# The last stage of a fused float32 kernel: two weight parts at a time, weights streamed in order of use, sums kept in PSUM, splits twice as wide

## The chip, the core and the metric

The kernel runs on one core of one Trainium2 chip. The metric is the device time of one execution in microseconds (us). TensorE multiplies (PE in the profile; its weight loads are PEld), VectorE (DVE), ScalarE (ACT) and GpSimd (POOL) work element by element, and SyncE (SP) issues the DMAs.

## What is computed

```python
x = attention(q, pooled k, pooled v)               # 8 batches x 576 tokens, 512 wide
x = ((x @ w1) * (x @ w2)) @ w3 @ w_out              # 4608 x 512
h = x @ w_in                                        # 512 -> 2048        the last stage
out = (h * sigmoid(1.702 * h)) @ w_out2             # 2048 -> 512
```

## The kernel before, in words

Only the last stage changes; everything before it issues the same instructions in both versions. Each float32 operand is kept as two parts, a rounded high part (a copy on ACT) and the rest (a subtraction on DVE): this pair of instructions is `split`, lines 104 and 105. A product is then three matmuls (high x high, high x low, low x high) of 128x128 weights with 512 moving columns: `mm3u`, line 706.

The stage takes nine blocks of 512 tokens. Block 0 is done plainly. The other eight are done as four **pairs** with a Strassen-Winograd scheme: each of the two layers needs seven products M1 to M7 in place of eight, with sums of the results between. A pair has two phases:

- The **first phase** (lines 922 to 973) loops over eight parts f of the hidden width. Per part each of M1 to M7 is 6 matmuls (two halves of 256 inputs, three matmuls each). Results are summed in four output blocks, go through gelu on ACT and become g11, g12, g22, g21; three differences of these are made on POOL (line 968). Between, M1 of the second layer runs, 12 matmuls for two parts (`m1_pair`).
- The **second phase** (lines 992 to 1039) runs the other six products of the second layer, 8 parts x 6 matmuls each. Its moving operands `mv` are splits of the g tiles, made by `make()` in a ring of NMV = 4 tiles, one part each.

Together a pair has 672 matmuls: 8 x 7 x 6 in the first phase and 7 x 8 x 6 in the second layer.

Weights come from DRAM in tiles `st` of 512 KB at most, in a ring of NST = 6 buffers: `stream()` lists them, and each `pull()` issues the next one on SP's queue, into the buffer used six tiles before. `win` tiles belong to the first layer, `wud` tiles to the second. While a pair's second phase runs, `x_prep` loads and splits the operands X of the next pair (tiles xM). Until the end of pair 1's first phase `w_sums` also prepares second-layer weights: load `u`, sums `ws`, and two results `wt` (cast on ACT, subtraction on DVE), each written to DRAM `wud` by DMA, from which later stages read it. A finished output is added and transposed on DVE into `ot` and stored.

A scheduler in the compiler's front end moves instructions on each engine's queue by its own estimate of times; a queue itself runs strictly in order.

## Time and profile before

| | us |
|---|---|
| median of three runs (lowest, highest) | 1592.86 (1592.41, 1598.03) |
| the profiled execution: its time, its span | 1596.34, 1594.6 |
| busy in the span: PE, PEld, DVE, ACT, POOL | 1476.6, 1200.8, 1033.9, 683.0, 672.0 |
| L706 waited until DVE's `mv` was done | 57.6 in 33 waits |
| L706 waited until DMAs of `st<-wud`, `st<-wind` landed | 48.3 in 25, 40.6 in 30 |

Matmuls overlap, so a busy PE may still run below its rate: a group of n matmuls is read by the distance from its start to the start of the next group. The granted clock (PEclk) is a share of 2.4 GHz; 0.5 is the lower level, 1.2 GHz.

### The profile page before, as it was taken

To read this page: it belongs to the slowest core of one execution; us is meant where nothing else is said; L and a number is where in the kernel's file an instruction comes from. 1 tells how busy PE (TensorE), PEld (TensorE's weight loads), DVE (VectorE), ACT (ScalarE), POOL (GpSimd) and SP (SyncE) were. 2 spreads that over 40 slices of the span, in tenths; PEclk is the share of its full clock that TensorE was granted. 3 is DMA by queue.
4 is the path that set the end of the run, shared out by engine and by line. 5 is a ranking of instruction groups with operands and counts; after the bars stand their busy time and mean duration, and the time that the engine had idled before them with its cause. 6 is when DMAs were issued, how large, how long until landed. Compare 5 with 4: busy or idle time off the path is not lost.

```text
span 1594.6 us, 19804 instructions
## 1 busy us (share of the span) xinstructions
PE 1476.6 (93%) x6536; PEld 1200.8 (75%) x6536; DVE 1033.9 (65%) x1868; ACT 683.0 (43%) x1304; POOL 672.0 (42%) x717
## 2 busy tenths in 40 slices
PE   5979999999999999999999888999879997999888
PEld 3757888888888888888887766777658775777766
DVE  7888997888778774556453568733495246843465
ACT  6974444333434343655442234422343234423333
POOL 8788765555554453659131234013230233103340
PEclk9999999999999999999999998999999998999999
DMA  9991323222323102998897776665557555665455
GB/s 279 231 205 33 88 57 59 66 68 56 71 46 78 39 35 76 326 341 288 287 392 213 248 251 190 204 198 172 187 173 205 176 168 184 185 201 165 159 178 139
DMA packets 290023, 267.67 MB, mean 168 GB/s; under 512 B 199296, under 2 KB 223872, under 8 KB 289920
## 3 DMA queue, kind: packets, MB, share of 16 engines
q1 hardware_dynamic: 289344, 265.35, 55.9%
q8 instruction: 52, 0.85, 0.2%
q10 hardware_dynamic: 576, 1.05, 0.2%
q14 instruction: 51, 0.42, 0.1%
HBM read 209.72 MB, written 56.62 MB: 167 GB/s over the span
## 4 chain that ended last, share of the span: by engine, by line
PE 71%; DMA 11%; DVE 11%; issue 2%; ACT 2%; POOL 1%; SPq 0%; DVEq 0%; ACTq 0%; POOLq 0%
PE bk L706 32%; PE wk L114 7%; PE wk L116 7%; PE wk L115 7%; DMA st<-wind 4%; PE acc L114 4%; PE acc L116 4%; PE acc L115 4%; DMA st<-wud 3%; DVE mv L105 2%; PE wk L278 2%; DVE xM L105 1%; DMA wud<-wt 1%; DMA m<-x2d 1%; POOL cv L172 1%
## 5 line engine op out<-in xcount | busy, mean ns | idle before, releaser
L706 PE MATMUL bk<-mv,st 128*128 128x512 f32 x1152 | 301.8, 419 | 47.7 <-DMA st<-wud 23.6
L706 PEld LDWEIGHTS bk<-mv,st 128*128 128x128 f32 x1152 | 231.4, 204 | 111.3 <-DMA st<-wud 24.7
L706 PE MATMUL bk<-xM,st 128*128 128x512 f32 x1056 | 255.6, 393 | 24.7 <-DMA st<-wind 20.0
L706 PEld LDWEIGHTS bk<-xM,st 128*128 128x128 f32 x1056 | 197.6, 189 | 75.2 <-DMA st<-wind 20.5
L114 PE MATMUL wk<-s,s 128*128 128x512 f32 x576 | 228.0, 397 | 6.4 <-DVE a L641 3.8
L116 PE MATMUL wk<-s,s 128*128 128x512 f32 x576 | 225.0, 391 | 1.0 <-DVE s L105 1.0
L115 PE MATMUL wk<-s,s 128*128 128x512 f32 x576 | 225.3, 392 | 0.1
L105 DVE TENSOR_TENSOR mv<-g,mv 128x512 fp32r<-128x512 f32 x192 | 151.3, 796 | 103.8 <-ACT mv L104 103.7
L314 DVE STREAM_TRANSPOSE p<-s_t 32x160 f32<-32x160 f32 (+1 forms) x560 | 178.5, 319 | 10.5
L968 POOL TENSOR_TENSOR g<-s,g 128x512 f32<-128x512 f32 x32 | 43.7, 1365 | 331.0 <-ACT s L849 329.7
L104 ACT CAST mv<-g 128x512 fp32r<-128x512 f32 x192 | 118.6, 620 | 106.9 <-PE bk L706 66.3
L116 PE MATMUL acc<-s,s 128*128 128x512 f32 x352 | 139.8, 397 | 2.0 <-DVE s L105 2.0
L115 PE MATMUL acc<-s,s 128*128 128x512 f32 x352 | 139.9, 397 | 1.3 <-POOL s L105 1.1
L114 PE MATMUL acc<-s,s 128*128 128x512 f32 x352 | 131.9, 400 | 8.1 <-DVE s L105 5.3
L105 POOL TENSOR_TENSOR s<-a,s 128x512 fp32r<-128x512 f32 x56 | 73.4, 1310 | 155.2 <-ACT s L104 121.4
L114 PEld LDWEIGHTS wk<-s,s 128*128 128x128 f32 x576 | 108.7, 189 | 30.8 <-DVE a L641 5.0
L116 PEld LDWEIGHTS wk<-s,s 128*128 128x128 f32 x576 | 108.4, 188 | 23.8 <-DVE s L105 1.2
L115 PEld LDWEIGHTS wk<-s,s 128*128 128x128 f32 x576 | 108.6, 189 | 22.2 <-DVE s L391 0.5
L172 POOL TENSOR_TENSOR cv<-cv,s 128x512 int32<-128x512 int32 x72 | 100.8, 1408 | 34.5 <-DVE cv L169 23.8
L968 POOL TENSOR_TENSOR g<-g,g 128x512 f32<-128x512 f32 x32 | 44.8, 1401 | 148.1 <-ACT g L849 147.1
L114 PEld LDWEIGHTS acc<-s,s 128*128 128x128 f32 x352 | 66.9, 191 | 22.9 <-ACT s L104 4.9
L116 PEld LDWEIGHTS acc<-s,s 128*128 128x128 f32 x352 | 67.1, 191 | 15.6 <-DVE s L105 2.9
(197 smaller groups left out, 2497.1 us busy)
## 6 DMA issues: line engine op xcount, KB each, us to landing
st<-wud SPq DMA_DIRECT2D x96, 512.0 KB, 4.0
st<-wind SPq DMA_DIRECT2D x85, 512.0 KB, 4.5
s<-in_moe_w_dram SPq DMA_DIRECT2D x32, 512.0 KB, 6.7
wind<-s SPq DMA_DIRECT2D x32, 512.0 KB, 5.4
s<-wind SPq DMA_DIRECT2D x27, 512.0 KB, 4.9
s<-in_moe_w_out_dram SPq DMA_DIRECT2D x24, 512.0 KB, 6.8
kr<-in_k_dram SPq DMA_DIRECT2D x128, 72.0 KB, 2.5
qr<-in_q_dram SPq DMA_DIRECT2D x128, 72.0 KB, 2.5
```

Source lines behind the costliest of these rows:

```text
L104: nc.scalar.copy(dst[:, 0], src)
L105: lo_eng.tensor_tensor(out=dst[:, 1], in0=src, in1=f32(dst[:, 0]), op=ALU.subtract)
L114: nc.tensor.matmul(o, a[:, 0, a_sl], b[:, 0, b_sl], start=first, stop=False)
L115: nc.tensor.matmul(o, a[:, 0, a_sl], b[:, 1, b_sl], start=False, stop=False)
L116: nc.tensor.matmul(o, a[:, 1, a_sl], b[:, 0, b_sl], start=False, stop=last)
L172: nc.gpsimd.tensor_tensor(out=w.bitcast(I32), in0=w.bitcast(I32), in1=lo_w.bitcast(I32), op=ALU.add)
L278: nc.tensor.matmul(sc[half][:, i * KW:(i + 1) * KW], qT[:, sl(tt)], mov, start=True, stop=True)
L314: nc.vector.transpose(out=dst[:, :nt, 32 * c:32 * c + 32], in_=s_t[32 * c:32 * c + 32, :nt, 32 * r:32 * r + 32])
L706: nc.tensor.matmul(o, w[:, x, m], b[:, y], start=first and n == 0, stop=last and n == 2, skip_group_check=True)
L968: nc.gpsimd.tensor_tensor(out=o, in0=p, in1=m, op=ALU.subtract)
```

## The change

The first phase takes two parts at once: index i is 0 or 1, and the order is the new `ORDER`, in which "O" is M1 of the second layer. M6, M7 and M4 add onto the PSUM bank of M1, and M3 onto that of M5; ACT copies the sum out after M1 (`m`), M6 (`u`) and M7 (`m`). DVE makes three sums per part where it made five. `mv`, and the tiles of g and X, hold two parts, so that casts, subtractions, gelu (but for g21) and POOL's differences work on 1024 columns; g21 has its difference with t2 in four instructions (`t4`) and not eight. Weight tiles are listed in the order of use; those of M7, M4 and M3 are filled by two DMAs of half the size, one per part. The second phase begins with M2 in place of M6. `x_prep` gives one step per group of 12 matmuls unless a step of an output (`late`) is due. `ot`, shared with `wt`, has one buffer in place of two; `ws` and the raw weights `wq` use tiles of g.

```diff
+                    n = 0
                     for src in srcs:
-                        nc.sync.dma_start(f32(t[:, :src.shape[1]]), src)
+                        nc.sync.dma_start(f32(t[:, n:n + src.shape[1]]), src)
+                        n += src.shape[1]
...
-            return pb.tile([P, 2, T], F32R, name="mv", tag=f"mv{i}")
+            return pb.tile([P, 2, 2, T], F32R, name="mv", tag=f"mv{i}")
...
-            return pb.tile([P, T // 32, 2, 32], F32, name="ot", tag="ot", bufs=2)
+            return pb.tile([P, T // 32, 2, 32], F32, name="ot", tag="ot")
...
-        ORDER = (("M1", A11, 0, True), ("M6", S2, 1, True), ("M5", S1, 2, True), ("M7", S3, 1, False),
-                 ("M2", A12, 0, False), ("M4", A22, 1, False), ("M3", S4, 2, False))
-        HS = {A11: (0, 0), A12: (0, 1), S1: (1, 0), S2: (1, 1), S3: (2, 0), S4: (2, 1), A22: (3, 0)}
-        OUT = (("M6", S2), ("M2", A12), ("M7", S3), ("M5", S1), ("M4", A22), ("M3", S4))
+        ORDER = (("M1", 0), ("M1", 1), ("M2", 0), ("M2", 1), ("M6", 0), ("M5", 0), ("M6", 1),
+                 ("M7", 0), ("M5", 1), ("M7", 1), ("M4", 0), ("O", 0), ("M4", 1), ("M3", 0),
+                 ("M3", 1))
+        PART = {"M1": ("a", 0), "M2": ("a", 1), "M5": ("s", 0), "M6": ("s", 1)}
+        OUT = (("M2", A12), ("M6", S2), ("M5", S1), ("M7", S3), ("M4", A22), ("M3", S4))
...
+            for fp in range(NFP):
+                fs = (2 * fp, 2 * fp + 1)
+                for f in fs:
+                    stream(("a", pr, f), win_d[f][:, A11:A12 + 1])
+                for f in fs:
+                    stream(("s", pr, f), win_d[f][:, S1:S2 + 1])
+                stream(("M7", pr, fp), *(win_d[f][:, S3:S3 + 1] for f in fs))
+                stream(("M4", pr, fp), *(win_d[f][:, A22:A22 + 1] for f in fs))
+                if fp < NFP - 1:
+                    stream(("o", pr, "M1", fp), wu_d[A11][:, 2 * fp:2 * fp + 2])
+                stream(("M3", pr, fp), *(win_d[f][:, S4:S4 + 1] for f in fs))
             for n, (name, u) in enumerate(OUT):
-                for f in range(0, NP1, 2):
-                    stream(("o", pr, name, f // 2), wu_d[u][:, f:f + 2])
-                    if n == 0 and f == 0:
-                        stream(("o", pr, "M1", NP1 // 2 - 1), wu_d[A11][:, NP1 - 2:])
+                for fp in range(NFP):
+                    stream(("o", pr, name, fp), wu_d[u][:, 2 * fp:2 * fp + 2])
+                    if n == 0 and fp == 0:
+                        stream(("o", pr, "M1", NFP - 1), wu_d[A11][:, NP1 - 2:])
...
+            def load():
+                for name in ("M1", "M7", "M2", "M3", "M5", "M6", "M4"):
+                    X[name] = pb.tile([P, 2, 2, T], F32R, name=f"x{name}", tag=f"x{name}")
+                for name, c, b in (("M1", 0, b0), ("M7", 0, b0 + 1), ("M3", 2, b0 + 1),
+                                   ("M2", 2, b0)):
+                    nc.sync.dma_start(lo(name), x2_d[b][:, c:c + 2])
...
+            def diff(j, name, p_, m_):
+                if j not in sums:
+                    sums[j] = pb.tile([P, T], F32, name="sx", tag="sx")
+                s = sums[j]
                 nc.vector.tensor_tensor(
...
+                    out=s, in0=lo(p_, j), in1=lo(m_, j) if m_ else s, op=ALU.subtract)
+                split(X[name][:, :, j], s, nc.vector)
+
+            steps = [load]
+            for j in range(2):
+                for args in (("M5", "M7", "M1"), ("M6", "M3", None), ("M4", "M2", None),
+                             ("M7", "M3", "M7")):
+                    steps.append(lambda j=j, args=args: diff(j, *args))
+            return steps + [lambda name=name: resplit(X[name], nc.vector)
+                            for name in ("M1", "M2", "M3")]
...
+                raw["w"] = pb.tile([P, 2, T], F32, name="wq", tag="g15")
...
-                c = raw["c"] = pb.tile([P, 4, HU], F32, name="ws", tag="ot", bufs=2)
+                c = raw["c"] = pb.tile([P, 4, HU], F32, name="ws", tag="g11")
...
-                t = pb.tile([P, 2, 2, HU], F32R, name="wt", tag="ot", bufs=2)
+                t = pb.tile([P, 2, 2, HU], F32R, name="wt", tag="ot")
...
-            if k >= 6 and k % 2 == 0 and len(wsum) > 4 * (NP1 - 2):
...
+                g11, g12, g22, g21, t2 = (gtile(a * NFP + fp) for a in range(5))
+                G.append((g11, g12, g22, g21, t2))
+                C, Z, W = [None] * 2, [None] * 2, [None] * 2
+                m1, U, V = [None] * 2, [None] * 2, [None] * 2
...
+                for name, i in ORDER:
+                    if name == "O":
+                        if fp < NFP - 1:
+                            if fp == 0:
+                                bA += [bank() for _ in range(2)]
+                            out_mm(bA, "M1", fp, fp == 0, False)
+                        continue
...
+                    bs = W if name == "M2" else Z if name in ("M5", "M3") else C
+                    first = name in ("M1", "M2", "M5")
+                    if first:
+                        bs[i] = bank()
...
                     if name == "M1":
-                        m1 = tmp("m1", 2)
-                        nc.scalar.copy(m1, o)
+                        m1[i] = tmp("m")
+                        nc.scalar.copy(m1[i], o)
+                    elif name == "M2":
+                        ready.pop(("a", pr, 2 * fp + i))
+                        pull()
+                        nc.vector.tensor_tensor(out=g11[:, i], in0=o, in1=m1[i], op=ALU.add)
+                        freed(W[i])
+                        if i:
+                            gelu(g11, g11)
+                            g = mvs["M1", fp] = moving()
+                            split(g, g11, nc.vector)
                     elif name == "M6":
-                        tt = tmp("tt", 1)
-                        nc.vector.tensor_tensor(out=tt, in0=o, in1=m1, op=ALU.add)
+                        U[i] = tmp("u")
+                        nc.scalar.copy(U[i], o)
                     elif name == "M5":
-                        if f and f % 2 == 0:
-                            m1_pair(f // 2 - 1)
+                        ready.pop(("s", pr, 2 * fp + i))
+                        pull()
                     elif name == "M7":
-                        q_ = tmp("q", 1)
-                        nc.vector.tensor_tensor(out=q_, in0=o, in1=m1, op=ALU.add)
-                        nc.vector.tensor_tensor(out=g22, in0=B[2][1], in1=q_, op=ALU.add)
-                        gelu(g22, g22)
+                        V[i] = tmp("m")
+                        nc.scalar.copy(V[i], o)
+                        nc.vector.tensor_tensor(out=g22[:, i], in0=Z[i][1], in1=V[i], op=ALU.add)
+                        if i:
+                            gelu(g22, g22)
+                    elif name == "M4":
+                        gelu(g21[:, i], o)
+                        freed(C[i])
+                    elif name == "M3":
+                        nc.vector.tensor_tensor(out=g12[:, i], in0=o, in1=U[i], op=ALU.add)
+                        freed(Z[i])
+                        if i:
+                            gelu(g12, g12)
+                    if i and name in ("M7", "M4", "M3"):
+                        ready.pop((name, pr, fp))
                         pull()
...
+                    if wsum and (name, i) in (("M2", 1), ("M5", 0), ("M7", 0), ("M4", 0),
+                                              ("M6", 1), ("M7", 1), ("M4", 1)):
+                        wsum.pop(0)()
...
+            src = {"M5": 0, "M7": 1, "M3": 2, "M2": 3, "M4": 3, "M6": 4}
+            todo_mv = [(name, fp) for name, _ in OUT for fp in range(NFP)]
+            t4 = list(range(NFP))
 
             def make():
                 if todo_mv:
...
+                    name, fp = todo_mv.pop(0)
+                    g = mvs[name, fp] = moving()
+                    split(g, G[fp][src[name]], nc.vector)
+                    if t4 and (name, fp) in (("M6", 0), ("M6", 2), ("M5", 0), ("M5", 2)):
+                        t = G[t4.pop(0)]
+                        nc.gpsimd.tensor_tensor(out=t[3], in0=t[3], in1=t[4], op=ALU.subtract)
...
+                bs = bW if name == "M2" else bZ if name in ("M5", "M3") else bA
+                for fp in range(NFP):
+                    out_mm(bs, name, fp, name in ("M2", "M5") and fp == 0, fp == NFP - 1)
+                    make()
+                    if name == "M2" and fp == 0:
+                        out_mm(bA, "M1", NFP - 1, False, True)
                         for m in range(2):
-                            m1.append(tmp("ma", 2))
+                            m1.append(tmp("m"))
                             nc.scalar.copy(m1[m], bA[m][1])
-                        for _ in range(NMV):
-                            make()
-                    elif name != "M6" or f:
                         make()
+                    if late:
+                        late.pop(0)()
+                    elif prep:
+                        prep.pop(0)()
```

**SP's queue in the first phase of pair 2**, before: tiles are `st` or `s4` with a number, wind2 and wind3 are parts f = 2 and 3, 128x1024 is a whole tile and 128x512 half of one.

```order
L700 DMA st_9695<-wind2_76 128x1024
L700 DMA st_9683<-wud0_98 128x1024
L700 DMA st_9641<-wind2_76 128x1024
L700 DMA s4_9631<-wind2_76 128x1024
L700 DMA st_9784<-wind3_77 128x512
L700 DMA st_9772<-wind3_77 128x1024
L700 DMA st_9715<-wind3_77 128x1024
L700 DMA st_9705<-wind2_76 128x512
L700 DMA s4_9760<-wind3_77 128x1024
L700 DMA st_9846<-wud0_98 128x1024
```

The same place now:

```order
L702 DMA st_9472<-wind2_76 128x1024
L702 DMA st_9498<-wind3_77 128x1024
L702 DMA st_9510<-wind2_76 128x1024
L702 DMA s4_9542<-wind2_76 128x512
L702 DMA s4_9542<-wind3_77 128x512
L702 DMA st_9533<-wind3_77 128x1024
L702 DMA st_9560<-wind2_76 128x512
L702 DMA st_9560<-wind3_77 128x512
L702 DMA st_9596<-wud0_98 128x1024
L702 DMA st_9606<-wind2_76 128x512
L702 DMA st_9606<-wind3_77 128x512
```

Before, the tile of M7 and M3 of part 2 (`st_9695`) is issued ahead of that of its M1 and M2 (`s4_9631`), and those of part 3's M4 and M7 (`st_9784`, `st_9772`) ahead of its M1's (`st_9715`). Now both tiles of M1 and M2, then those of M5 and M6, M7, M4, wud0 and M3 follow each other nearly as they are used.

**DVE's queue where pair 2 passes to its second phase**, before, from the last sum of the first phase on (m1, q, tt, xM belong to the next pair's `x_prep`):

```order
L963 TENSOR_TENSOR g7_10138<-bk1_10137,tt_10154 128x512
L105 TENSOR_TENSOR xM30_10421<-q_10276,xM30_10421 128x512
L105 TENSOR_TENSOR mv_10295<-g8_9575,mv_10295 128x512
L778 TENSOR_TENSOR m1_10270<-m1_10272,m1_10270 128x512
L105 TENSOR_TENSOR mv_10307<-g9_9650,mv_10307 128x512
L778 TENSOR_TENSOR m1_10272<-q_10276,m1_10272 128x512
L105 TENSOR_TENSOR xM50_10351<-m1_10270,xM50_10351 128x512
L105 TENSOR_TENSOR mv_10346<-g12_9887,mv_10346 128x512
L778 TENSOR_TENSOR q_10276<-q_10276,m1_10270 128x512
L105 TENSOR_TENSOR xM20_10495<-tt_10274,xM20_10495 128x512
L105 TENSOR_TENSOR xM70_10389<-m1_10272,xM70_10389 128x512
L105 TENSOR_TENSOR mv_10286<-g19_10051,mv_10286 128x512
```

Now, from the same sum on (sx and xM are `x_prep`, `m` and `ot` the output of M2; mv_10058 is the fourth tile of M2, mv_10108, mv_10128 and mv_10150 the second, third and fourth of M6):

```order
L976 TENSOR_TENSOR g7_9877<-bk3_9958,u_9947 128x512
L105 TENSOR_TENSOR mv_10058<-g15_9879,mv_10058 128x1024
L105 TENSOR_TENSOR mv_10108<-g17_9570,mv_10108 128x1024
L792 TENSOR_TENSOR sx_10090<-xM3_10064,sx_10090 128x512
L105 TENSOR_TENSOR mv_10128<-g18_9725,mv_10128 128x1024
L105 TENSOR_TENSOR xM6_10066<-sx_10090,xM6_10066 128x512
L1017 TENSOR_TENSOR m_10054<-bk0_10021,m_10054 128x512
L792 TENSOR_TENSOR sx_10090<-xM2_10063,sx_10090 128x512
L730 STREAM_TRANSPOSE ot_10135<-m_10054 128x16x32
L1017 TENSOR_TENSOR m_10056<-bk1_10022,m_10056 128x512
L105 TENSOR_TENSOR mv_10150<-g19_9880,mv_10150 128x1024
```

Four splits of 512 columns stood among seven instructions of `x_prep`; now four of 1024 stand among three of `x_prep` and three of an output, and the first tiles of M2 and of M6 are made further ahead.

**TensorE's queue at the same place now**, behind the last M3 (its first row): the rest of M1, then M2 (bk0, bk1) with the first tile of M6 (bk6, bk7) between; five matmuls of that tile follow, and then M6's second tile, mv_10108.

```order
L709 MATMUL bk3_9958<-xM3_8937,s4_9906 128x512 x6
L709 MATMUL bk7_9520<-mv_9921,st_9939 128x512 x2
L709 MATMUL bk0_10021<-mv_10018,st_9965 128x512 x6
L709 MATMUL bk1_10022<-mv_10018,st_9965 128x512 x6
L709 MATMUL bk0_10021<-mv_10037,st_9977 128x512 x6
L709 MATMUL bk1_10022<-mv_10037,st_9977 128x512 x6
L709 MATMUL bk0_10021<-mv_10058,st_9993 128x512
L709 MATMUL bk1_10022<-mv_10058,st_9993 128x512
L709 MATMUL bk6_9519<-mv_10086,s4_10010 128x512 x6
L709 MATMUL bk7_9520<-mv_10086,s4_10010 128x512
L709 MATMUL bk0_10021<-mv_10058,st_9993 128x512 x5
L709 MATMUL bk1_10022<-mv_10058,st_9993 128x512 x5
```

Before, M6 stood first, on a source that POOL's last difference gives; now M2 does, on g21.

**ACT's queue in pair 1's first phase now**; a `wt` cast needs the one buffer that the one before filled and DMA emptied:

```order
L831 CAST wt_8354<-ws_8323 128x2x256
L968 COPY m_8472<-bk6_8385 128x512
L968 COPY m_8495<-bk7_8394 128x512
L858 ACTIVATE g9_8382<-g9_8382 128x1024
L831 CAST wt_8428<-ws_8323 128x2x256
L950 COPY m_8578<-bk4_8571 128x512
L858 ACTIVATE g13_8383<-bk6_8385 128x512
L858 ACTIVATE g13_8383<-bk7_8394 128x512
L104 CAST mv_8891<-g13_8383 128x1024
L831 CAST wt_8475<-ws_8461 128x2x256
```

Ten such casts stand among the copies and gelus of the second to the fourth two parts; before, twelve stood in the phase, with two buffers that they shared with `ws` and `ot`.

## Rows read from the trace of the kernel before

**Rows 1.** Timeline of PE: start, length, group of matmuls, count, idle before it.

```profile
857.38 7.87 PE L706 MATMUL bk<-xM,st 128*128 128x512 f32 x34
1201.40 13.76 PE L706 MATMUL bk<-mv,st 128*128 128x512 f32 x60
1215.00 2.88 PE L706 MATMUL bk<-mv,s 128*128 128x512 f32 x12
1579.28 8.32 PE L706 MATMUL bk<-mv,st 128*128 128x512 f32 x36
```

**Rows 2.** Engines by stretch: length, busy (count) of PE, PEld, DVE, ACT, POOL; PEclk, DMA.

```profile
1049.00:1136.00 87.00, 77.74 (x336) 62.16 (x334) 33.09 (x47) 27.48 (x46) 25.65 (x19) 1.00 0.59 184
1150.00:1185.00 35.00, 25.24 (x91) 18.28 (x90) 32.42 (x38) 16.77 (x30) 17.18 (x11) 0.90 0.55 175
1185.00:1219.00 34.00, 34.00 (x150) 27.82 (x149) 24.34 (x39) 15.53 (x25) 0.00 (x0) 1.00 0.75 217
1519.00:1546.00 27.00, 22.71 (x83) 16.85 (x83) 18.21 (x18) 9.37 (x16) 16.91 (x11) 0.87 0.45 149
```

**Rows 3.** Timeline of PE, pairs 1 and 2: single waits.

```profile
934.62 1.61 PE L706 MATMUL bk<-xM,st 128*128 128x512 f32 x6 [1.69 <-DVE tt L941]
...
1088.59 9.80 PE L706 MATMUL bk<-xM,st 128*128 128x512 f32 x42 [1.00 <-DMA st<-wind]
...
1136.83 4.59 PE L706 MATMUL bk<-mv,st 128*128 128x512 f32 x12 [3.07 <-DMA st<-wud]
...
1165.41 4.04 PE L706 MATMUL bk<-mv,st 128*128 128x512 f32 x10 [3.34 <-DVE mv L105]
```

**Rows 4.** Timeline of SP's queue: the issue before that wait for wud.

```profile
1132.42 0.32 SPq L700 DMA_DIRECT2D st<-wud  x1
```

**Rows 5.** DMA issues: out<-in, count, KB each, median us to landing.

```profile
st<-wud SPq DMA_DIRECT2D x96, 512.0 KB, 4.0
st<-wind SPq DMA_DIRECT2D x85, 512.0 KB, 4.5
...
wud<-wt SPq DMA_DIRECT2D x32, 256.0 KB, 4.4
st<-wind SPq DMA_DIRECT2D x32, 256.0 KB, 3.5
```

**Rows 6.** Timeline of DVE in pair 2, then of POOL there.

```profile
1156.12 1.77 DVE L105 TENSOR_TENSOR mv<-g,mv 128x512 fp32r<-128x512 f32 x1
...
1186.59 1.88 DVE L105 TENSOR_TENSOR mv<-g,mv 128x512 fp32r<-128x512 f32 x3
...
1155.61 1.74 POOL L968 TENSOR_TENSOR g<-g,g 128x512 f32<-128x512 f32 x1
1157.30 1.75 POOL L968 TENSOR_TENSOR g<-g 128x512 f32<-128x512 f32 x1
```

**Rows 7.** Single lines: duration ns lowest/median/highest, first and last start.

```profile
L968 POOL TENSOR_TENSOR g<-g,g x32: 1261/1287/1737, 934.0 to 1523.9; 128x512 f32<-128x512 f32 x32
L1023 DVE TENSOR_TENSOR u<-bk,ma x8: 675/677/678, 987.6 to 1532.8; 128x512 f32<-128x512 f32 x8
L104 ACT CAST mv<-g x192: 602/622/627, 865.7 to 1582.2; 128x512 fp32r<-128x512 f32 x192
L938 ACT COPY m<-bk x32: 581/589/590, 858.7 to 1492.6; 128x512 f32<-128x512 f32 x32
```

**Rows 8.** Timeline of ACT in pair 1's first phase: the `wt` casts, first and last four.

```profile
864.35 0.62 ACT L822 CAST wt<-ws 128x512 fp32r<-128x512 f32 x1 [0.97 <-DMA out_dram<-ot]
...
925.25 0.62 ACT L822 CAST wt<-ws 128x512 fp32r<-128x512 f32 x1 [2.91 <-DMA wud<-wt]
931.29 0.62 ACT L822 CAST wt<-ws 128x512 fp32r<-128x512 f32 x1 [3.90 <-DMA wud<-wt]
937.14 0.62 ACT L822 CAST wt<-ws 128x512 fp32r<-128x512 f32 x1 [2.20 <-DMA wud<-wt]
943.05 0.62 ACT L822 CAST wt<-ws 128x512 fp32r<-128x512 f32 x1 [1.17 <-DMA wud<-wt]
```

More of the change, by code (lines that the diff above doesn't have):

```diff
@@ L906, in pooled_attention_moe_moe2, with out_mm @@
             X = xc.pop(pr)
[L907 to L908 removed]
+            bA = []
+            G = []
             mvs = {}
[L911 to L912 removed]
+            def out_mm(bs, name, fp, first, last):
+                g, w = mvs.pop((name, fp)), ready.pop(("o", pr, name, fp))
                 for m in range(2):
[L914 to L920 removed]
@@ L922, in pooled_attention_moe_moe2 @@
-            for f in range(NP1):
-                B = [bank() for _ in range(3)]
-                ga.append(gtile(f))
-                gb.append(gtile(NP1 + f))
-                if f % 2 == 0:
-                    gc.append(gtile(2 * NP1 + f // 2))
-                g12, g22, g11, g21 = ga[f][:, 0], ga[f][:, 1], gb[f][:, 0], gb[f][:, 1]
-                t2 = gc[f // 2][:, f % 2]
-                for name, u, b, first in ORDER:
-                    o = B[b][1]
-                    s, h = HS[u]
-                    w = ready["h", pr, f, s]
+                    for i in range(2):
+                        mm3u(bs[m][1], w[:, i], m, g[:, :, i], first and i == 0, last and i == 1)
@@ L971, in pooled_attention_moe_moe2 @@
[L971 to L973 removed]
+            while wsum:
+                wsum.pop(0)()
             prep = x_prep(pr + 1) if pr < NPAIR else []
[L977 to L980 removed]
+            src = {"M5": 0, "M7": 1, "M3": 2, "M2": 3, "M4": 3, "M6": 4}
@@ new lines, in pooled_attention_moe_moe2, with out_of, part, end @@
+            late = []
+            def out_of(name, bs):
+                ot = out_tile()
+                add, blk, i = {"M2": (m1, b0, 0), "M7": (V, b1, 1),
+                               "M4": (None, b0, 1), "M3": (U, b1, 0)}[name]
+                def part(m):
+                    if add:
+                        nc.vector.tensor_tensor(out=add[m], in0=bs[m][1], in1=add[m], op=ALU.add)
+                    turn_out(ot, m, add[m] if add else bs[m][1])
+                def end():
+                    part(1)
+                    store(ot, blk, i)
+                return [lambda: part(0), end]
@@ L1040, in pooled_attention_moe_moe2 @@
+                        nc.scalar.copy(V[m], bA[m][1])
+                if name in ("M2", "M7", "M4", "M3"):
+                    late += out_of(name, bZ if name == "M7" else bs)
+                if name == "M2":
+                    freed(*bW)
+                elif name == "M4":
+                    freed(*bA)
+            while late:
+                late.pop(0)()
+            freed(*bZ)
             while prep:
```

140 lines of the change are left out of this document (27 added, 113 removed).

## The prediction

> **What bounds the kernel now.** I read the timeline of TensorE first. The last stage's four pairs begin at 857.38 and their last matmul group begins at 1579.28 and ends at 1587.60, so they take 730.2 us [rows 1]. Where nothing waits, 60 matmuls take 1215.00 - 1201.40 = 13.60 us, 0.2267 us each, at full clock [rows 1]. Four pairs of 672, less the one that had run before 857.38, are 2687 matmuls: 609.1 us. TensorE is the bound, and 121.1 us of these stages, 30 a pair, are not its work. An earlier stage cannot change, as its queues are the same.
>
> The table by stretch shows where pair 2 loses its share [rows 2]. Its first phase ran 336 matmuls (76.2 us) in 87.0: 10.8 lost. The start of the second phase ran 91 (20.6 us) in 35.0: 14.4 lost. After that 150 matmuls took 34.0, which is the price: nothing lost. The rest of the 30, some 5 us, goes where the phases meet. Pair 4 has no next pair to prepare; its start lost 27.0 - 83 x 0.2267 = 8.2.
>
> Then the single waits [rows 3]. In the first phase TensorE waits about 1 us at a time for `st<-wind`, and 3.07 us for `st<-wud` at 1136.83. SP issued that tile only at 1132.42 [rows 4]; a tile lands in 4.0 to 4.5 us [rows 5], so it was late because its buffer came free late, not because the transfer was slow. At the second phase's start TensorE waits for `mv` from DVE, 3.34 us once, and behind that wait 10 matmuls took 4.04 us where the price is 2.3 [rows 3]: the stretch from 1150 to 1185 has a granted clock of 0.90 [rows 2], so after such waits part of the work ran at the lower level of 1.2 GHz. A wait removed gives more than its own length.
>
> **What the change does to each.**
>
> *Weights in the first phase.* The six buffers now go round in order of use. The tightest tile is the first of M1: its buffer comes free when M5 has used it, and from there to its use lie some 25 matmuls, 5.7 us, against 4.5 us to land [rows 5]. The others have 36 matmuls (8.2 us) or more. The half-size DMAs are priced by the 256 KB row, 3.5 us [rows 5]; two issued one behind the other stay under 8.2. So the waits for `st` go to nothing. Bound on the other side: they stay as they are, 10.8 us a pair.
>
> *Sums in PSUM.* Three hand-offs per part now go from TensorE to ACT and back: the copies of M1, M6 and M7 must be out before the bank is added to. A copy takes 0.59 us [rows 7]; at least two other products, 12 matmuls or 2.7 us, stand between in the new order. Cost nothing; what hides it is that order, and ACT being free. ACT's first-phase work for two parts is 8 instructions of 0.59 to 0.62 us and four double ones of at most 1.24 [rows 7], at most 10 us in 21.8 (96 matmuls). DVE has six sums of 0.68 us [rows 7] and two double splits, below 7 us.
>
> *The second phase's start.* M2 goes first, on g21, which is long there, so the wait for POOL's last difference goes. What is late next is M6. I take the end of the last M3 as time 0 and go down the queues. TensorE: the new order puts 50 matmuls before M6's second tile (due at 11.3), 12 more before the third (14.1), and 77 before the low part of the fourth (17.5). DVE: a split of 512 columns takes 0.60 (three in 1.88 [rows 6]), a double one at most 1.2. POOL: 1.29 a difference [rows 7], doubled at most 2.6, I take 2.4; four of them run from 3.4 on. And DVE and POOL wait for each other: a split that meets a POOL difference took 1.77, POOL's own took 1.74, in turns [rows 6], while DVE sums that read PSUM never took over 0.68 [rows 7]. So each SBUF instruction of DVE waits for the POOL one that runs. In turns this gives: M2's fourth tile done at 3.4, M6's second at 7.0, `sx` at 9.9, M6's third at 13.4 (due 14.1), then one subtraction behind the fourth difference at 16.3, four instructions of the output and `sx` without POOL to 18.7, M6's fourth at 19.9: 2.4 late. From there DVE needs 2.4 us per group of 2.72 and catches up. Taken: 2.5 us in each of pairs 1 to 3, 0 in pair 4, which has no `x_prep`. Ends: 0, and the 14.4 of today.
>
> The Trainium skill states the same in "SBUF — State Buffer", section "SBUF: two separate sides": GpSimd and a VectorE instruction with two SBUF inputs take a shared pair of ports as an exclusive lock for the whole instruction, and the other blocks fully. The rows agree (1.77 against 0.60). By that rule wide differences speak against this change, as each holds the lock twice as long: were all four to block a split that is due, a start would lose 4 x 2.4 = 9.6 in place of 2.5, and the forecast below would be 21 us higher, 1519.
>
> *One buffer for `wt`.* In pair 1 a cast must wait until DMA has emptied the buffer: cast 0.62 [rows 8], subtraction as long as a sum, 0.68 [rows 7], two issues of 0.32 [rows 4], landing 4.4 [rows 5], 6.4 us with the hand-offs. Today, with two buffers shared, the last casts came every 5.9 us and the twelve of the phase took 864.35 to 943.05, on average 7.2 [rows 8]. Now ten of them stand in ACT's queue from the second two parts on, about 24 us into the phase (96 matmuls and the gelus behind them): the tenth falls at 24 + 9 x 6.4 = 81.6, while TensorE, unhindered, wants the copies behind it after 315 matmuls, at 71. ACT is in order, so M1, M6 and M7 of the last two parts queue behind it: 11 us lost, in pair 1 alone. Ends: 0 (6 us cycles, slack at the copies) and 22.
>
> *The rest.* One buffer for `ot` is emptied between two outputs 10.9 us apart; nothing. X is ready early, since `x_prep` now ends some 10 groups before the pair does. The tail after the last matmul keeps its two sums, two transposes and a store. Small waits at phase changes remain: my estimate is 2 us a pair of the 5 that go there today, 8 in all.
>
> **The sum.** 121.1 goes; 11 + 3 x 2.5 + 8 = 26.5 stays or is new: 94.6 less than the profiled execution's 1596.3, which is 1501.7. The median stands 3.5 below that execution, so I forecast **1498 us**.
>
> **Rivals.**
>
> 1. *Everything hidden.* The `wt` casts find slack and the locks fall between: 10 us remain of 121, giving 1593 - 111 = 1482. For it: after 1185 the second phase loses nothing today [rows 2]. Against: ten serial round trips.
> 2. *DVE and POOL keep the start of the second phase as it is.* Turns at twice the width cost as much as today, 3 x 14.4 + 8.2 = 51, with `wt` and small waits 70: 1593 - 51 = 1542. For it: DVE is busy 32.4 of 35.0 us there [rows 2]. Against: today that stretch has far more of `x_prep`. This is the case that the lock rule of that page supports.
> 3. *Slower: the hand-offs to ACT.* Six copies per two parts, 96 in the four pairs, and TensorE may not go on with a bank until ACT has copied it. The nearest row for such a hand-off that fails is 1.69 us, where M7 had to wait for a DVE sum that M6's bank needed [rows 3]. If ACT's queue, held by a cast or gelu of twice the width, left each hand-off uncovered by that much, 96 x 1.69 = 162 us would come and 121 go: 1634. It decides from 121 / 96 = 1.26 us per hand-off. Against it: 2.7 us of other matmuls before each.
> 4. *The first phase keeps its weight waits*, since DMAs land slower in halves: 43 us of the gain gone, 1541; with half of rival 2 1560.
>
> **How the numbers follow.** The forecast (1487 to 1520) has 0.50, everything hidden (below 1487) 0.14, rivals 2 and 4 (1520 to 1560) 0.26, no change 0.04, slower by the hand-offs 0.06. The measurement can tell about 0.5%, 8 us. So faster 0.90, same 0.04, slower 0.06. The range of 8 in 10 leaves out the slow cases (0.10), the top of rivals 2 and 4, and a little below: 1478 to 1545. The likeliest case's own range is 1487 to 1520; its ends are the bounds of `wt` (0 to 22) and some 10 us of locks.
>
> **What would show it.** Right: no wait for `st` of over 0.5 us in the first phases of pairs 2 to 4; pairs 2 and 3 take 156 to 160 us each; pair 1 is the longest by about 10, its waits ending on ACT's copies behind a `wt` cast that waits for `wud<-wt`; PEclk 1.00 in most of the stretch. Wrong: DVE splits of over 3 us beside POOL and a TensorE wait for `mv` in the second phase of over 5 us (rival 2); TensorE waiting for ACT `m` or `u` in every part (rival 3); waits for `st<-wind` (rival 4).

## The result and the profile after

The changed kernel takes **1496.72 us** (median of 4 runs, 1491.15 to 1500.06) against 1593.47 us for the kernel before: a ratio of 0.9384, with a 95% interval of 0.935 to 0.9418. The profiled execution took 1496.2 us, its span 1494.0.

The timeline of PE, rows that answer to [rows 1]: the first matmul group of each pair, then the last group.

```profile
856.46 5.38 PE L709 MATMUL bk<-xM,st 128*128 128x512 f32 x23
...
1023.85 1.52 PE L709 MATMUL bk<-xM,s 128*128 128x512 f32 x6
...
1179.86 11.04 PE L709 MATMUL bk<-xM,st 128*128 128x512 f32 x48
...
1335.36 5.60 PE L709 MATMUL bk<-xM,st 128*128 128x512 f32 x24
...
1474.08 13.76 PE L709 MATMUL bk<-mv,st 128*128 128x512 f32 x60
```

The four pairs take 631.4 us in place of 730.2. At 152.3 us of matmuls a pair (672 at 0.2267 us) the loss, which is the time of a pair above its matmuls, is now 15.1 us in pair 1, 3.7 in pair 2, 3.2 in pair 3 and 0.2 in pair 4: 22 in place of 121.

The table by stretch, as in [rows 2]: pair 2's first phase up to its only wait, the start of its second phase, and pair 4's start.

```profile
1024.00:1099.00 75.00, 75.00 (x333) 62.12 (x332) 25.21 (x29) 30.82 (x42) 26.26 (x11) 1.00 0.65 196
...
1115.00:1150.00 35.00, 33.49 (x147) 27.19 (x146) 32.02 (x31) 19.51 (x25) 11.90 (x4) 1.00 0.73 235
...
1425.00:1452.00 27.00, 27.00 (x121) 22.37 (x120) 19.68 (x15) 13.06 (x14) 11.46 (x4) 1.00 0.77 242
```

333 matmuls in 75.0 us of the first phase are the price and no more; before, 336 took 87.0. The start of the second phase does 147 matmuls in 35 us where it did 91, at full clock, though DVE is as busy as before (32.02 of 35 us).

The waits that are left, in the timeline of PE (idle time and its releaser in brackets), where before had those of [rows 3]:

```profile
890.09 0.70 PE L709 MATMUL bk<-mv,s 128*128 128x512 f32 x2 [1.05 <-DMA s<-wud]
...
912.90 1.66 PE L709 MATMUL bk<-xM,s 128*128 128x512 f32 x6 [0.80 <-ACT u L962]
...
920.28 4.63 PE L709 MATMUL bk<-mv,st 128*128 128x512 f32 x10 [3.89 <-DVE mv L105]
...
943.56 1.65 PE L709 MATMUL bk<-xM,st 128*128 128x512 f32 x6 [1.89 <-ACT u L962]
...
975.84 0.51 PE L709 MATMUL bk<-mv,st 128*128 128x512 f32 x1 [1.62 <-ACT mv L104]
...
1102.89 3.00 PE L709 MATMUL bk<-mv,st 128*128 128x512 f32 x12 [1.35 <-DMA st<-wud]
1133.46 0.50 PE L709 MATMUL bk<-mv,st 128*128 128x512 f32 x1 [1.28 <-ACT mv L104]
1134.19 7.75 PE L709 MATMUL bk<-mv,st 128*128 128x512 f32 x33 [0.23 <-DVE mv L105]
```

Pair 3 repeats the last three (0.81, 1.23 and 0.23). Pair 1 has the longest wait, and the 10 matmuls behind it took 4.63 us, twice the price: part of the stretch ran at the lower clock level, as its row in the table by stretch shows (0.82).

```profile
908.00:925.00 17.00, 12.30 (x44) 9.35 (x43) 10.51 (x9) 6.13 (x9) 9.94 (x4) 0.82 0.71 244
```

What held DVE and ACT there? Their timelines, ACT's first, then DVE's, then POOL's:

```profile
910.79 0.62 ACT L831 CAST wt<-ws 128x512 fp32r<-128x512 f32 x1 [3.02 <-DMA wud<-wt]
...
911.45 1.81 DVE L832 TENSOR_TENSOR wt<-ws,wt 128x512 fp32r<-128x512 f32 x1 [3.64 <-ACT wt L831]
913.29 5.00 DVE L826 TENSOR_TENSOR ws<-wq 128x256 f32<-128x256 f32 x2
...
919.01 1.22 DVE L105 TENSOR_TENSOR mv<-s,mv 128x1024 fp32r<-128x1024 f32 x1
...
912.66 2.86 POOL L987 TENSOR_TENSOR g<-g,g 128x1024 f32<-128x1024 f32 x1
...
915.48 2.54 POOL L1004 TENSOR_TENSOR g<-g,g 128x1024 f32<-128x1024 f32 x1
```

The split that TensorE waits for (919.01) is short. It is late because two sums of only 256 columns stood before it and took 2.5 us each: by the rows, each of them waited until a POOL instruction had ended. The same pair of sums took 0.76 us where POOL did nothing (the row of 918.34 below). But the sums also came late to POOL: the `wt` subtraction ahead of them had waited 3.64 us for its cast, and the cast 3.02 us for `wud<-wt`. The rows alone do not tell which of the two made the loss; the runs below take each away.

The wait of 1.89 us at 943.56 has another origin. M6's copy stood on ACT behind a cast of the next pair's X, which waited for its load:

```profile
939.56 1.05 ACT L109 CAST xM<-xM 128x1024 fp32r<-128x1024 f32 x1 [4.92 <-DMA xM<-x2d]
```

### The profile page after: what moved, and what is told of

Its sections match the earlier page's. It is cut to its first block, busy times and chain, and to the rows that moved or that the text cites. A ratio compares the mean times of both kernels' runs of the same rounds, so it can differ in the third digit from the quotient of the medians.

```text
span 1494.0 us, 19448 instructions
## 1 busy us (share of the span) xinstructions
PE 1441.0 (96%) x6536; PEld 1189.5 (80%) x6536; DVE 962.9 (64%) x1664; ACT 693.8 (46%) x1212; POOL 662.1 (44%) x653
## 3 DMA queue, kind: packets, MB, share of 16 engines
q10 hardware_dynamic: 576, 1.05, 0.2%
## 4 chain that ended last, share of the span: by engine, by line
PE 83%; DVE 6%; DMA 5%; ACT 2%; issue 2%; POOL 2%; SPq 0%; DVEq 0%; POOLq 0%; ACTq 0%
PE bk L709 38%; PE wk L114 8%; PE wk L116 8%; PE wk L115 8%; PE acc L114 5%; PE acc L116 4%; PE acc L115 4%; PE wk L278 2%; DMA xM<-x2d 2%; PE bk L115 1%; PE bk L116 1%; PE bk L114 1%; POOL cv L172 1%; DVE p L314 1%; DMA st<-wud 1%
## 5 line engine op out<-in xcount | busy, mean ns | idle before, releaser
L709 PE MATMUL bk<-mv,st 128*128 128x512 f32 x1104 | 263.6, 394 | 9.6 <-DVE mv L105 4.6
L709 PE MATMUL bk<-xM,st 128*128 128x512 f32 x1140 | 268.4, 390 | 1.9 <-ACT u L962 1.9
L709 PEld LDWEIGHTS bk<-mv,st 128*128 128x128 f32 x1104 | 209.2, 190 | 56.3 <-DVE mv L105 5.9
L709 PEld LDWEIGHTS bk<-xM,st 128*128 128x128 f32 x1140 | 214.4, 188 | 46.9 <-ACT u L962 2.3
L987 POOL TENSOR_TENSOR s<-g,s 128x1024 f32<-128x1024 f32 x16 | 38.8, 2423 | 426.0 <-ACT g L858 426.0
L105 DVE TENSOR_TENSOR mv<-g,mv 128x1024 fp32r<-128x1024 f32 x80 | 112.9, 1411 | 43.8 <-ACT mv L104 42.6
L104 ACT CAST mv<-g 128x1024 fp32r<-128x1024 f32 x80 | 84.1, 1053 | 64.9 <-PE bk L709 62.3
L114 PEld LDWEIGHTS acc<-s,s 128*128 128x128 f32 x352 | 66.7, 190 | 22.2 <-ACT s L104 5.0
L116 PEld LDWEIGHTS acc<-s,s 128*128 128x128 f32 x352 | 66.8, 190 | 15.6 <-DVE s L105 3.0
L115 PEld LDWEIGHTS acc<-s,s 128*128 128x128 f32 x352 | 66.8, 190 | 14.5 <-POOL s L105 2.3
```

Of the source, the lines that this page charges most:

```text
L104: nc.scalar.copy(dst[:, 0], src)
L105: lo_eng.tensor_tensor(out=dst[:, 1], in0=src, in1=f32(dst[:, 0]), op=ALU.subtract)
L114: nc.tensor.matmul(o, a[:, 0, a_sl], b[:, 0, b_sl], start=first, stop=False)
L115: nc.tensor.matmul(o, a[:, 0, a_sl], b[:, 1, b_sl], start=False, stop=False)
L116: nc.tensor.matmul(o, a[:, 1, a_sl], b[:, 0, b_sl], start=False, stop=last)
L709: nc.tensor.matmul(o, w[:, x, m], b[:, y], start=first and n == 0, stop=last and n == 2, skip_group_check=True)
```

## The experiments

Length of the four pairs in each profiled run, from the first group of a pair to that of the next, the last to the end of its matmuls (us), with the ratio to the kernel before in the timed runs. Every edit also lets the scheduler arrange the queues anew: pairs 2 and 3 gained 2.4 to 2.9 us in copies_doubled, which only adds work. So a difference of a few us in a pair needs its rows beside it:

| kernel | pair 1 | pair 2 | pair 3 | pair 4 | ratio (95%) |
|---|---|---|---|---|---|
| before | 180.4 | 181.3 | 184.6 | 183.9 | 1 |
| changed | 167.4 | 156.0 | 155.5 | 152.5 | 0.9384 (0.935 to 0.9418) |
| wt_two | 167.7 | 155.4 | 157.0 | 152.5 | 0.9409 (0.9383 to 0.9434) |
| diffs_on_dve | 157.5 | 153.1 | 153.2 | 153.3 | 0.9331 (0.9302 to 0.936) |
| dve_wt_two | 153.0 | 154.6 | 153.5 | 153.2 | 0.9293 (0.9269 to 0.9316) |
| copies_doubled | 171.3 | 153.1 | 153.1 | 152.5 | 0.9401 (0.9375 to 0.9427) |
| three_moving | 162.2 | 160.5 | 162.0 | 160.6 | 0.9489 (0.9466 to 0.9512) |
| m6_first | 171.0 | 160.3 | 160.0 | 154.1 | 0.9474 (0.9447 to 0.9502) |
| m6_first_late | 171.7 | 166.4 | 166.0 | 155.5 | 0.9556 (0.9527 to 0.9585) |
| before_in_order | 173.6 | 177.0 | 174.7 | 171.9 | 0.9797 (0.9764 to 0.983) |
| before_dve | 169.6 | 176.4 | 178.4 | 176.9 | 0.9843 (0.9811 to 0.9876) |
| before_order_dve | 171.6 | 173.2 | 171.8 | 171.7 | 0.9744 (0.9721 to 0.9767) |

**A second `wt` buffer** (wt_two).

```diff
-                t = pb.tile([P, 2, 2, HU], F32R, name="wt", tag="ot")
+                wt_n[0] += 1
+                t = pb.tile([P, 2, 2, HU], F32R, name="wt",
+                            tag="g19" if wt_n[0] > 6 and wt_n[0] % 2 else "ot")
```

> The changed kernel with a second buffer for `wt` in pair 1 (the tile of the last `t2`, which is free until then). Theory, step of the `wt` buffer: the ten casts that wait for `wud<-wt` cost pair 1 its 11 us. Then the three waits of pair 1 that the changed kernel shows between 908 and 945 (0.80, 3.89 and 1.89 us, with the slower matmuls behind them) go, pair 1 falls from 167.4 us to about 156, and the time from 1496.7 to about 1486: a ratio of 0.932 to the kernel before. Rival: the buffer is not what is short. The 3.89 us came from two `ws` sums on DVE that took 5.00 us together beside POOL's differences, and the 1.89 us from a cast on ACT that waited 4.92 us for the next x. Then only the 0.80 us and some of the slow matmuls go: pair 1 stays at 165 to 167 us, ratio 0.937 to 0.938.

1497.88 us, and pair 1 stays at 167.7: the rival. No `wt` cast of this pair waits for `wud<-wt` any more, and yet nothing is gained, so the theory of the buffer falls as the cause of the 11 us. The sums of weights come earlier and meet POOL elsewhere. DVE's timeline, then PE's:

```profile
884.85 5.05 DVE L828 TENSOR_TENSOR ws<-wq 128x256 f32<-128x256 f32 x2
...
890.16 0.68 DVE L958 TENSOR_TENSOR s<-bk,m 128x512 f32<-128x512 f32 x1
...
894.50 2.67 PE L709 MATMUL bk<-xM,st 128*128 128x512 f32 x6 [4.27 <-ACT u L966]
```

The sum `s<-bk,m` reads PSUM and takes its usual 0.68, but it stands behind the sums of weights, ACT's gelu behind it, and M6's copy behind the gelu.

**The differences on DVE** (diffs_on_dve): no work on POOL in these stages.

```diff
-                    nc.gpsimd.tensor_tensor(out=o, in0=p, in1=m, op=ALU.subtract)
+                    nc.vector.tensor_tensor(out=o, in0=p, in1=m, op=ALU.subtract)
...
-                        nc.gpsimd.tensor_tensor(out=t[3], in0=t[3], in1=t[4], op=ALU.subtract)
+                        nc.vector.tensor_tensor(out=t[3], in0=t[3], in1=t[4], op=ALU.subtract)
```

> The changed kernel with all its differences (three per two parts and the fourth of the second phase) on DVE in place of POOL: 16 more instructions of 1.2 us on DVE in each pair, which is busy about 80 of 152 us there. Theory of the lock: DVE's instructions between SBUF tiles took 1.70 to 3.42 us beside POOL's differences at the second phase's start of pair 2, in place of 0.68 and 1.2, 6.6 us more in all there, while the four differences on DVE itself take 4.8. Then every DVE instruction is back at its short time, the waits of 1.5 us for `mv` at 1133 and 1289 and the 3.89 us in pair 1 go, pairs 2 and 3 take about 154.5 us each, and the ratio is 0.930 to 0.936. Rival: DVE's queue is what is short at that start, whoever does the differences: its 16 more instructions push the splits back, TensorE's waits for `mv` grow to 3 us or more per pair, pairs 2 and 3 take 157 to 160 us, ratio 0.940 to 0.945.

1485.27 us: the theory of the lock, by the time. Pair 1 falls by 9.9 us, pairs 2 and 3 by 2.9 and 2.3, though DVE has 16 instructions more in each; pair 4 grows by 0.8. In pairs 2 and 3 the waits for `mv` go (1.51 and 1.46 us), but so do those for `st<-wud` (1.35 and 0.81), which the lock does not explain; copies_doubled below bears on both. DVE's timeline in pair 1, then ACT's and PE's, and the stretch by engines where pair 2's second phase starts:

```profile
914.30 1.22 DVE L1004 TENSOR_TENSOR g<-g,g 128x1024 f32<-128x1024 f32 x1
...
918.34 0.76 DVE L826 TENSOR_TENSOR ws<-wq 128x256 f32<-128x256 f32 x2
...
916.96 0.62 ACT L831 CAST wt<-ws 128x512 fp32r<-128x512 f32 x1 [2.65 <-DMA wud<-wt]
...
918.12 2.65 PE L709 MATMUL bk<-xM,s 128*128 128x512 f32 x6 [1.70 <-ACT u L962]
...
1107.00:1142.00 35.00, 35.00 (x156) 28.91 (x155) 32.52 (x37) 20.96 (x25) 0.00 (x0) 1.00 0.77 244
```

The wait of 1.70 us that remains is the one that I had forecast: M6's copy behind a `wt` cast behind `wud<-wt`. In the last row DVE is busy 32.52 of 35 us with the four differences among its work, where it was busy 32.02 without them: part of its busy time had been waiting for POOL.

**Both** (dve_wt_two).

> The changed kernel with its differences on DVE and the second `wt` buffer together. With the differences on DVE alone pair 1 took 157.5 us, 5 more than the 152.3 of its matmuls, with a wait of 1.70 us for a copy on ACT that stood behind a `wt` cast, which had waited 2.65 us for `wud<-wt`. Theory: now that no difference on POOL holds DVE's sums, the one buffer is what is left of pair 1's loss, and with two it falls to about 154 us; ratio 0.930 to 0.931 against 0.933. Rival: the second buffer did nothing by itself and does nothing here: pair 1 stays at 157 to 158 us, ratio 0.933.

1479.85 us, the fastest of all. Pair 1 is at 153.0, with a single wait left, of 0.56 us: in the profiled executions the second buffer is worth 4.5 us once POOL's differences are gone, and nothing before that. The ratios' intervals of the two runs overlap, so the timed runs alone would not show it.

**Copies from PSUM twice** (copies_doubled).

```diff
-                        nc.scalar.copy(U[i], o)
+                        for _ in range(2):
+                            nc.scalar.copy(U[i], o)
```

and the same for M1 and M7.

> The changed kernel with each copy of M1, M6 and M7 from PSUM in the first phases made twice, one after the other: 24 more ACT instructions of 0.59 us in each pair, 96 in all, each in the way of a bank that TensorE wants to add to. Theory, step of the sums in PSUM: at least 2.7 us of other matmuls cover each hand-off, so 1.2 us in place of 0.59 is covered too. Pairs 2 to 4 grow by less than 1 us each; pair 1, where ACT's queue also holds the `wt` casts, by up to 4: ratio 0.938 to 0.942. Rival 3, the hand-offs lie on the path: every copy shows with its 0.59 us, 57 us in all, some 14 us in each pair, 1553 us, ratio 0.974 to 0.976.

1495.80 us. Pairs 2 to 4 do not grow, pair 1 by 3.9: the hand-offs are covered. In pair 1 the sums of weights now meet POOL twice (4.99 us at 888.05, 4.96 at 917.75), and TensorE's longest wait stands behind the second meeting; whether the copies or the new order of the queues brought that about was not tested. DVE in pair 1, then PE there and at the start of pair 2's second phase:

```profile
917.75 4.96 DVE L826 TENSOR_TENSOR ws<-wq 128x256 f32<-128x256 f32 x2
...
926.73 1.22 PE L709 MATMUL bk<-mv,st 128*128 128x512 f32 x2 [7.16 <-ACT mv L104]
...
1135.66 8.23 PE L709 MATMUL bk<-mv,st 128*128 128x512 f32 x35 [0.41 <-DVE mv L105]
```

Pairs 2 and 3 take 153.1 us, as in diffs_on_dve, with POOL's differences where they were: M6's fourth tile is late by only 0.41 us, as DVE's queue has another order and its splits beside POOL take 2.20 us where the changed kernel's took 3.42, and no wait for `st<-wud` stands there. So what diffs_on_dve gains in pairs 2 and 3 can also be had from a different order, and is not shown to be the lock's alone. Pair 1's gain is another matter: with POOL's differences pair 1 took 162.2 us or more in every run of the changed kernel, and 157.5 and 153.0 without.

**Three moving tiles** (three_moving): `NST, NMV = 6, 3`, and the split that follows M2's first tile moved behind M1's last part, since three tiles leave no room ahead of it.

> The changed kernel with three moving tiles in place of four. Before, four tiles of 6 matmuls held 5.4 us of TensorE's work; the changed kernel's four of 12 hold 10.9 us, three hold 8.2. Theory of the look-ahead: the start of the second phase is easy now because DVE may run twice as far ahead; with 2.7 us less of it M6's fourth tile is later by up to that, pairs 2 and 3 take 157.5 to 159 us, pair 4 up to 2 more, ratio 0.942 to 0.946. Rival: the tiles are not what DVE waits for there; its queue and its turns with POOL are, and nothing moves by more than 1 us a pair, ratio 0.938 to 0.941.

1510.85 us, 14 more: the time falls outside both forecasts, and on the side of the look-ahead. DVE in pair 2, then PE:

```profile
1123.13 2.84 DVE L792 TENSOR_TENSOR sx<-xM,sx 128x512 f32<-128x512 f32 x1 [4.66 <-DMA xM<-x2d]
1125.90 3.37 DVE L105 TENSOR_TENSOR mv<-g,mv 128x1024 fp32r<-128x1024 f32 x1
...
1129.32 4.09 PE L709 MATMUL bk<-mv,s 128*128 128x512 f32 x10 [5.07 <-DVE mv L105]
```

The wait for the split that POOL stretches is 5.07 us where four tiles leave 1.5. Not all of it is POOL's: with one split less made ahead, the split stands behind an `sx` of `x_prep`, and DVE was idle 4.66 us there until a load of x landed. Pair 1 is 5 us shorter: in its first phase no pair of `ws` sums takes over 2.84 us, where the changed kernel has one of 5.00, and no wait of TensorE is over 1.83.

**M6 before M2** (m6_first, m6_first_late). The second phase has its old beginning, M1's last part ahead of both. In m6_first M2 reads two of its four `g21` tiles after `t2` is taken off them, so that kernel computes something else; m6_first_late mends that with the last two lines of the cut.

```diff
-        OUT = (("M2", A12), ("M6", S2), ("M5", S1), ("M7", S3), ("M4", A22), ("M3", S4))
+        OUT = (("M6", S2), ("M2", A12), ("M5", S1), ("M7", S3), ("M4", A22), ("M3", S4))
...
+            out_mm(bA, "M1", NFP - 1, False, True)
...
-                    if t4 and (name, fp) in (("M6", 0), ("M6", 2), ("M5", 0), ("M5", 2)):
+                    if t4 and (name, fp) in (("M2", 1), ("M2", 3), ("M5", 0), ("M5", 2)):
```

> The changed kernel with the old beginning of the second phase: M1's last part, then M6, then M2. Theory, step of the second phase's start: with M2 first nothing waits for POOL's last differences. With M6 first its fourth tile needs the last `t2`, which POOL finished 9 us after the first phase's last matmul in pair 2 of the changed kernel (1123.9 against 1114.8), and a split beside POOL takes 2 to 3 us more, against a due time of 10.9 us; and M1's sum must be copied out (about 1 us with nothing between). So each start loses some 3 to 4 us where it now loses 1.5 in pairs 2 and 3 and nothing in pair 4: the part behind the first phase takes 67 to 69 us in pairs 2 and 3 in place of 65.1, 66 in pair 4 in place of 63.0, 8 to 14 us in all, ratio 0.944 to 0.948. Rival: which product goes first does not matter, since the wider tiles hold twice as much work for TensorE ahead: those parts stay within 1 us, ratio 0.938 to 0.941.

> The run with M6 ahead of M2 again, now with the fourth differences (`g21` less `t2`) behind M2's splits, as M2 needs `g21` whole; the run before took them ahead of M2's splits, and M2 read other values. Theory, unchanged: the start waits for the last `t2` and for M1's copy, and loses 8 us in each pair as in that run (70 us behind the first phase in place of 65.1), ratio 0.945 to 0.950. Rival: part of that loss came from POOL taking the fourth differences in the middle of M6; with them later the loss halves, 67 us behind the first phase in pairs 2 and 3, ratio 0.941 to 0.944.

1508.72 and 1525.08 us: 12 us more, within the first theory's range, and 28 with the fourth differences where they must then be, which is more than the second said. So M2 first is worth 28 us against the old beginning that computes the same; the two runs differ only in the place of the fourth differences, so that place accounts for the 16 us between them. In the second run POOL, then DVE, then PE in pair 2:

```profile
1126.56 3.25 POOL L987 TENSOR_TENSOR g<-g,s 128x1024 f32<-128x1024 f32 x1
...
1130.28 3.37 DVE L105 TENSOR_TENSOR mv<-g,mv 128x1024 fp32r<-128x1024 f32 x1
...
1133.70 5.07 PE L709 MATMUL bk<-mv,st 128*128 128x512 f32 x14 [3.07 <-DVE mv L105]
```

**Parts of the change in the kernel before.** The weights in order of use (before_in_order):

```diff
-                for i, (a, b) in enumerate(((A11, A12), (S1, S2), (S3, S4), (A22, A22))):
-                    stream(("h", pr, f, i), win_d[f][:, a:b + 1])
...
+            uses = [(f, u) for f in range(NP1) for _, u, _, _ in ORDER]
+            for n in range(0, len(uses), 2):
...
+                stream(("h", pr, n // 2), *(win_d[f][:, u:u + 1] for f, u in uses[n:n + 2]))
```

> The kernel before with one part of the change alone: the first phase's weights streamed in the order of their use (two pieces of 256 KB in a buffer, next to each other in that order, a buffer refilled once both are used). One part at a time, sums on DVE, splits of 512 columns and the second phase stay as they were. Theory, step of the weights: the first phase of pair 2 lost 10.8 us, nearly all of it to waits for weights, 43 us over four pairs; waits for `st<-wind` (40.6 us in 30 before) nearly vanish and the time falls by some 43 us to 1550, ratio 0.973. Rival: the order of the weights alone does little, because the waits go over to what is late next in that phase, the DVE sums that free the banks (1.69 us once before) and the splits: ratio 0.99 to 1.00, with the same loss in the first phase put down to DVE.

1559.87 us against 1590.96, 31 less where the theory said 43. Its table by stretch, pair 2's first phase and the start of the second, then two of TensorE's waits in the whole run (what for, us in total, times):

```profile
1031.00:1120.00 89.00, 87.17 (x377) 69.90 (x376) 34.78 (x51) 28.71 (x48) 23.27 (x18) 1.00 0.63 190
...
1136.00:1171.00 35.00, 23.81 (x82) 17.84 (x81) 29.03 (x34) 16.08 (x28) 17.18 (x11) 0.80 0.50 155
...
ACT xM L104: 25.9, 5
DMA st<-wind: 13.8, 11
```

377 matmuls in 89.0 us lose 3.5 where 336 lost 10.8. The waits for `st<-wind` fall from 40.6 to 13.8 us and do not vanish. The start of the second phase is as bad as before or worse (82 matmuls, 16.4 lost), and TensorE's waits for casts of X come to 25.9 us in five waits, where the kernel before lists none: part of the gain is given back there.

The differences on DVE (before_dve), the edit of diffs_on_dve in the older code:

> The kernel before with all its differences on DVE in place of POOL. In pair 2 from 1150 to 1185 DVE was busy 32.4 of 35.0 us with 38 instructions, 25 us of them at their short time and 7 us more by turns with POOL; POOL's 11 differences there would add 7.5 us to DVE at 0.68 each. Theory that DVE has too much to do there, with the whole x preparation (21 of its 38 instructions) in that stretch: no relief, the start of the second phase still loses 13 to 16 us in pairs 1 to 3, and the time is within 1% of before, ratio 0.99 to 1.00. Rival, the lock alone holds TensorE up: with no turns the start loses half or less (7 us or under), and pair 4 too, 25 us or more in all, ratio 0.985 or under.

1567.67 us against 1593.02: the rival by the time, though not quite in its place. Pair 1 gains 10.8 us, the others 5 to 7; the start in pair 2 (119 matmuls from 1145 to 1180) still loses 8.0 us where it lost 14.4. TensorE's waits for `mv` from DVE fall from 57.6 to 33.3 us in the whole run.

Both (before_order_dve):

> The kernel before with its first phase's weights in the order of their use and all its differences on DVE: the two edits that gave 0.980 and 0.984 alone. If each takes its own waits away, they add: 31 + 25 us, ratio 0.964 to 0.967, 1537 us, and the 52 us from there to the changed kernel with its differences on DVE (0.933) are what M2 first, the wider look-ahead and the sums in PSUM bring. Rival: they share waits (what the one takes away the other would have hidden, or DVE, now with all the work, becomes late in a first phase that runs faster): 0.972 to 0.980.

1555.35 us against 1595.86, 40 less where the two alone sum to 56: they share waits. What is left shows on DVE and PE in pair 2:

```profile
1143.85 0.69 DVE L780 TENSOR_TENSOR m<-m,m 128x512 f32<-128x512 f32 x1 [2.91 <-DMA m<-x2d]
...
1145.06 0.69 DVE L105 TENSOR_TENSOR mv<-g,mv 128x512 fp32r<-128x512 f32 x1
...
1145.20 5.46 PE L708 MATMUL bk<-mv,s 128*128 128x512 f32 x12 [4.23 <-ACT xM L104]
```

A subtraction of the x preparation waits 2.91 us for its load, and the split of a moving tile stands behind it on DVE. By the profile TensorE's wait of 4.23 us ends with ACT's cast of what that subtraction gave.

## Why the prediction was right, and where not

The forecast was 1498 us and the sum holds: 22 us remain of 121 where it had 26.5, and pair by pair 15.5, 4.5, 4.5 and 2 were forecast and 15.1, 3.7, 3.2 and 0.2 measured. One of its causes was wrong, and that pair 1 agrees to 0.4 us is luck.

*Weights in the first phase*: right in mechanism. No wait for `st<-wind` is left, and the order alone, put into the kernel before, takes most of that phase's loss away. It was too absolute: `st<-wud` still waits 1.35 and 0.81 us. SP's queue, then the chain of waits (start, length, what), then the DMA issues (KB each, median us to landing):

```profile
1096.58 0.32 SPq L702 DMA_DIRECT2D st<-wud  x1
1096.99 0.44 SPq L784 DMA_DIRECT2D xM<-x2d  x1
```

```profile
1096.58 6.17 DMA st<-wud
```

```profile
st<-wud SPq DMA_DIRECT2D x92, 512.0 KB, 4.2
...
xM<-x2d SPq DMA_DIRECT2D x16, 512.0 KB, 6.9
```

That tile was issued next to a load of x, and its transfer took 6.17 us, while TensorE wanted it 5.0 us after its issue; the term took 4.5 for every tile, and 5.7 at the least to its use. That the load of x made it slow was not tested.

*Sums in PSUM at no cost*: right. With 96 copies doubled the time stayed within the spread of the runs, where rival 3 asked for 57 us more, and in pairs 2 to 4 of the changed kernel TensorE nowhere waits for `m` or `u`. So rival 3 is out.

*The second phase's start*: right in place and nearly in size. M6's fourth tile is late by 1.84, 1.51 and 1.46 us in pairs 1 to 3 where 2.5 was forecast, and not at all in pair 4. The walk down DVE's queue holds step by step: counted from the end of the last M3 at 1114.79, M6's second, third and fourth tiles were done at 6.9, 13.0 and 19.4 where 7.0, 13.4 and 19.9 were forecast. DVE's rows there, and POOL's:

```profile
1119.31 2.34 DVE L105 TENSOR_TENSOR mv<-g,mv 128x1024 fp32r<-128x1024 f32 x1 [1.00 <-ACT mv L104]
...
1124.39 3.42 DVE L105 TENSOR_TENSOR mv<-g,mv 128x1024 fp32r<-128x1024 f32 x1
...
1132.94 1.20 DVE L105 TENSOR_TENSOR mv<-g,mv 128x1024 fp32r<-128x1024 f32 x1
...
1123.88 2.85 POOL L987 TENSOR_TENSOR g<-g,g 128x1024 f32<-128x1024 f32 x1
```

The split at 1124.39 waits out POOL's instruction and then runs: 3.42 in place of 1.2 us. The Trainium skill says this in "SBUF — State Buffer", section "SBUF: two separate sides" (a lock held for a whole instruction), and the row agrees. That the turns cost the start so little rests on two parts of the change: M2 first (12 to 28 us when undone) and moving tiles that hold 10.9 us of work (14 us with one fewer, loads of x included). The step named only the first of these. It rests on the order of DVE's queue too, as copies_doubled shows (0.41 late in place of 1.51).

*One buffer for `wt`*: this step failed, although its 11 us were met by chance. It put the loss of pair 1 down to ten round trips through one buffer. Its sign, a wait that ends on ACT's copies behind a `wt` cast behind `wud<-wt`, stands in the trace once, with 0.80 us. With two buffers pair 1 is the same; with POOL's differences gone it loses 10 us less; and only then do two buffers take off 4.5 more. So the larger cause was the turns of DVE and POOL, and the buffer costs only where these are gone. The step before had worked out the turns, but applied them to the second phase alone: the sums of weights in pair 1's first phase also read SBUF on both sides and meet POOL's wide differences. The prediction's count of DVE's work in a first phase (six sums and two double splits) left these sums out.

*The rest*: 8 us were set aside for small waits, and X was called ready early. By the timeline pair 1's first phase loses 11 us: 3.89 for the split and some 2.2 by which the ten matmuls behind it ran over their price, 1.89 behind the load of x, 1.05 for weights, 0.80 behind the `wt` cast, and small gaps. Its second phase's start loses 4: waits of 1.84 in all, and matmuls over their price around them. So the loads of x were not free; a floor of 2 us a pair was too high for pair 4 (0.2).

Where the 97 us came from can be said only in part. Weights in order: 31 alone. M2 first 28 (12 in the kernel that computes something else), look-ahead 14, each by taking it back. Such parts need not add, as before_order_dve shows, and what the sums in PSUM save by themselves was not measured.

## What to carry to other kernels

When two engines take turns on a port, go through every stage where both work, and look for what is queued behind the shorter instruction: a sum of 0.4 us that takes 2.5 holds up all that follows on its engine. A forecast that meets the time can have the wrong cause; only the run that takes the suspected cause away tells, and it may have to be taken away together with another that hides it. Moving POOL's work to a DVE that was already busy 32 of 35 us at one stretch made the kernel faster and left that share at 32.5: the busy time of an engine that waits for a port is not all work, and what counted in pair 1 was how long a single instruction could hold the queue.
